# A second level of Strassen's algorithm for two of the seven products of a tiled GEMM, with a new order of its sums

## The chip, the cores and the metric

The kernel runs on one core of one Trainium2 chip. The metric is the device time of one execution in microseconds (us); for a comparison the median of several executions is taken. The core's engines are called as in the profile: PE is TensorE (matrix products), PEld its weight loads, DVE is VectorE, ACT is ScalarE, POOL is GpSimd, and SP issues the DMAs. Matrix products are written to banks of PSUM, the other tiles lie in SBUF.

## The reference

A retention recurrence over 4 sequences of 768 tokens and 8 heads of 64 gives a matrix x of 3072 x 512, and a layer with an ELU between two GEMMs follows. All is in 32 bits.

```
state = gamma[h] * state + outer(k[t], v[t])            # per sequence and head, 64 x 64
y[t]  = (q[t] @ state) / sqrt(64)
x     = y as (3072, 512)
h     = x @ w_in                                        # 512 x 2048
g     = where(h > 0, h, exp(min(h, 0)) - 1)
out   = g @ w_out                                       # 2048 x 512
```

## The kernel before

**Blocks.** The tokens go in six blocks (`tb` = 0 to 5) of 512. Block 0 is computed plainly (`plain_first`, `plain_second`), while the weights arrive and are decoded. From block 1 on both GEMMs use Strassen's algorithm in Winograd's form: the operands are cut into 2 x 2 quarters, and seven products M1 to M7 of combined quarters take the place of eight. The weights' combinations are made once (`combine_w_in` for the first GEMM, `combine_w_out` for the second), the inputs' once per block (`combine_x` makes four from `xb`, the retention's result).

**First GEMM.** `first(n)` computes a quarter of the hidden units, n = 0 to 3; in each, a product is four matmuls of 128x256 into one bank (line 497). `strassen` gives the order M1, M2, M6, M7, M5, M3, M4 and where the sums fall. Products that share a sum accumulate in one PSUM bank: M1, M6, M5 and M3 follow one another in bank `a`, and what stood there is taken out between two of them by a copy on ACT (`kept`, line 447). Bank `a` has two buffers, `b` and `d` one each. The sums C11, C12, C21 and C22 go through the ELU: two activations on ACT (lines 373 and 374) and one operation on DVE (line 376), which `elu` puts into the list `later`, so that it is issued with the next ELU. Combinations T1 and T3 of the results follow (line 509). The last two products of an n are run in the next n, or between products of the second GEMM.

**Second GEMM.** Block 1 uses `second`, one level of Strassen. Blocks 2 to 5 use `second_twice`: there every one of the seven products is itself cut into seven small products [1] to [7] of four matmuls of 128x128 each (line 618). The small weights come from DRAM through a ring of 11 buffers of 256 KB (`fetch_small`, lines 594 and 597), in the order of the list `to_fetch`: those that are quarters from `scratch`, those that are sums from `scratch2`, which `combine_w_out` filled during block 1. The ring and the inputs' pool `tpool` take the memory of the pools `stage` and `t4`, which are closed when block 1 is done. Between the products of the second GEMM the retention of the next block is done in five steps (`retention_step`), and its `combine_x` stands behind the last product's begin (`behind_last`).

**What sets the order.** The program is written in its final order; nothing reorders it. The generators `strassen`, `second_twice` and `inner` are stepped by hand in the loop at the end:

```
    for tb in range(1, NTB):
        for n in range(NQ):
            cur = first(n)
            for at in range(3):
                next(cur)
            for _ in tail:
                pass
            ...
            tail = cur
            if more:
                load((tb + 1) * CPB + n)
                scale_v((tb + 1) * CPB + n)
```

All DMAs are issued by SP in program order. Scaling v by the decay (`scale_v`, line 239) is POOL's only work from block 1 on.

Of the kernel before, what the change touches and what calls it, by code (L numbers as in the profile page):

```python
# [2 lines left out]

# [5 lines left out]
FP32 = mybir.dt.float32  # L9
# [3 lines left out]
ALU = mybir.AluOpType  # L13
# [3 lines left out]
def kernel(  # L17
# [3 lines left out]
    w_bits: bass.AP,  # L21
    scratch: bass.AP,
    scratch2: bass.AP,
    out: bass.AP,
    dims,
):

# [74 lines left out]

    w_a = [const.tile([P, 2, 2, 2, P], FP32, name=f"w_a{n}") for n in range(NQ)]
    w_b = [const.tile([P, 2, 2, 2, P], FP32, name=f"w_b{n}") for n in range(NQ)]
    w_s = [const.tile([P, 3, 2, 2, P], FP32, name=f"w_s{n}") for n in range(NQ)]
    NPIECE = 2 * NQ + NF  # L110
    staged, prepared, decoded = [], [], []

# [109 lines left out]


    xb = const.tile([P, 4, TB], FP32, name="xb")
    xt = [const.tile([P, 2, TH], FP32, name=f"xt{n}") for n in range(4)]
    carry = [const.tile([P, HP, D], FP32, name=f"carry{n}") for n in range(2)]
    held = {}

# [123 lines left out]

    half = [slice(0, TH), slice(TH, TB)]

    def combine_x():
        sub = lambda o, x, y: nc.vector.tensor_tensor(out=o, in0=x, in1=y, op=ALU.subtract)
        b11, b12, b21, b22 = (xb[:, 2 * r : 2 * r + 2, half[t]] for r in range(2) for t in range(2))
        sub(xt[0], b12, b11)
        sub(xt[1], b22, xt[0])
        sub(xt[2], b22, b12)  # L360
        sub(xt[3], b21, xt[1])


    later = []

    def flush():
        while later:
            later.pop(0)()

    def elu(g, h):  # L370

        r = epool.tile([P, 512], FP32, name="r", tag="r")
        nc.scalar.activation(r, h, AF.Relu, scale=-1.0)  # L373
        nc.scalar.activation(r, r, AF.Exp, scale=-1.0)  # L374
        flush()
        later.append(lambda: nc.vector.scalar_tensor_tensor(g, r, -1.0, h, ALU.add, ALU.max))  # L376

    def plain_first():

# [62 lines left out]
    def bank(x):  # L442
        return ps_f.tile([P, 2, TH], FP32, name="p" + x, tag=x, bufs=2 if x == "a" else 1)
# [103 lines left out]
                scratch2[j - 1, :, 1024 * k : 1024 * k + 1024], x.rearrange("p k f d -> p (k f d)")  # L547
            )

    def second(tb):  # L550
        def product(j, ps, begin):
            ws = fetched.pop((tb, j))
            for f in range(NF):
                for d in range(2):
                    nc.tensor.matmul(  # L555
                        ps[:, d, :], lhsT=ws[:, 2 * d + f // 4, f % 4, :], rhs=gq[INPUT2[j]][:, f, :],
                        start=(begin and f == 0 and d == 0), stop=(f == NF - 1), skip_group_check=True,
                    )
            at = ORDER2.index(j) + 3
            if j in (2, 6):  # L560
                next_input(j)
            combine_w_out(j, ws)
            if at < 7:
                fetch(tb, ORDER2[at])

        def use(name, h):
            r, t = int(name[1]) - 1, int(name[2]) - 1
            if name == "C12":
                ot = hpool.tile([P, 2, TH], FP32, name="h", tag="h")
                nc.scalar.copy(ot, h)  # L570
                h = ot
            nc.sync.dma_start(out[tb, r, t].rearrange("p d c -> p (d c)"), h.rearrange("p d c -> p (d c)"))

        return strassen(product, use, None)
# [1 line left out]


    RING = 11
    USE = [(1, k) for k in (1, 2, 6, 7, 5)]
    for at in range(1, 7):  # L580
        j, before = ORDER2[at], ORDER2[at - 1]
        USE += [(j, 1), (j, 2), (before, 3), (before, 4), (j, 6), (j, 7), (j, 5)]
    USE += [(4, 3), (4, 4)]
    to_fetch = [(tb, j, k) for tb in range(2, NTB) for j, k in USE]
    small_w = []

    def fetch_small():
        if not to_fetch:
            return
        tb, j, k = to_fetch.pop(0)  # L590
        t = ring.tile([P, 4, P], FP32, name="wq", tag="wq")
        if k in (1, 2, 4):
            q = 4 * SLOT[j] + {1: 0, 2: 1, 4: 3}[k]
            nc.sync.dma_start(t.rearrange("p f d -> p (f d)"), scratch[q])
        else:
            n = {5: 0, 6: 1, 7: 2, 3: 3}[k]
            nc.sync.dma_start(t.rearrange("p f d -> p (f d)"), scratch2[j - 1, :, 512 * n : 512 * n + 512])
        small_w.append(((tb, j, k), t))

    def second_twice(tb, behind_last):  # L600
        quarter = lambda x, r, t: x[:, 4 * r : 4 * r + 4, P * t : P * t + P]
        ts, kept2 = {}, {}

        def inputs(j):
            x, t = gq[INPUT2[j]], tpool.tile([P, 4, 4, P], FP32, name="ts", tag="ts")
            b11, b12, b21, b22 = (quarter(x, a, b) for a in range(2) for b in range(2))
            sub = lambda o, x, y: nc.vector.tensor_tensor(out=o, in0=x, in1=y, op=ALU.subtract)
            sub(t[:, 0], b12, b11)
            sub(t[:, 1], b22, t[:, 0])
            sub(t[:, 2], b22, b12)  # L610
            sub(t[:, 3], b21, t[:, 1])
            ts[j] = {1: b11, 2: b21, 3: b22, 4: t[:, 3], 5: t[:, 0], 6: t[:, 1], 7: t[:, 2]}

        def product(j, k, ps, begin):
            name, w = small_w.pop(0)
            assert name == (tb, j, k)
            for f in range(4):
                nc.tensor.matmul(  # L618
                    ps, lhsT=w[:, f, :], rhs=ts[j][k][:, f, :], start=(begin and f == 0), stop=(f == 3),
                    skip_group_check=True,  # L620
                )
            fetch_small()
# [9 lines left out]
        def inner(j):  # L632
            pool, tag = (mpool, "m") if j in (1, 6, 7, 5) else (hpool, "h")
            res = pool.tile([P, 2, 2, P], FP32, name="res", tag=tag)
            pa = bank("a")[:, 0, 0:P]
            product(j, 1, pa, True)
            m1 = copy(pa)
            pb = bank("b")[:, 0, 0:P]
            product(j, 2, pb, True)
            add(res[:, 0, 0], pb, m1)  # L640
            yield
            product(j, 6, pa, False)
            u2 = copy(pa)
            pd = bank("d")[:, 0, 0:P]
            product(j, 7, pd, True)
            yield
            product(j, 5, pa, False)
            add(res[:, 1, 1], pd, copy(pa))
            yield
            product(j, 3, pa, False)  # L650
            nc.scalar.copy(res[:, 0, 1], pa)
            product(j, 4, pd, False)
            add(res[:, 1, 0], pd, u2)
            sum_up(j, res.rearrange("p d t c -> p (d t c)"))
# [23 lines left out]
                add(m, kept2[7], m)  # L678
                store("C21", m)

        inputs(1)
        before = iter(())
        for at, j in enumerate(ORDER2):
            cur = inner(j)
# [3 lines left out]
            for _ in before:  # L688
                pass
            if j == 2:  # L690
                next_input(2)
            if j == 5:
                next_input(6)
# [12 lines left out]
            before = cur  # L706
            yield j
        for _ in before:
            pass


    prepare(2)
# [51 lines left out]
            for _ in combine_w_in(0):  # L764
                pass
    combine_x()
    for j in ORDER2[:3]:
        fetch(1, j)


    def retention_step(tb, step):
# [8 lines left out]
        elif step < 5:  # L780
            outputs_step(tb, step - 2)

    tail = iter(())
    for tb in range(1, NTB):
        more = tb + 1 < NTB
        for n in range(NQ):
            cur = first(n)
            for at in range(3):
                next(cur)

            for _ in tail:
                pass
            side = combine_w_in(n + 1) if tb == 1 and n + 1 < NQ else iter(())
            for s in cur:
                next(side, None)
                if s == "gap":
                    break
            for _ in side:
                pass
            tail = cur  # L800
            if more:
                load((tb + 1) * CPB + n)
                scale_v((tb + 1) * CPB + n)
        if tb == 1:
            cur = second(tb)
            next(cur)
            next(cur)
            for _ in tail:
                pass
            flush()  # L810
            for step, s in enumerate(cur):
                retention_step(tb + 1, step)
            combine_x()
            tail = iter(())
            early.close()
            ring = ctx.enter_context(tc.tile_pool(name="ring", bufs=RING))
            tpool = ctx.enter_context(tc.tile_pool(name="tpool", bufs=2))
            for _ in range(RING):
                fetch_small()
        else:  # L820
            cur = second_twice(tb, combine_x if more else lambda: None)
            next(cur)
            for s in tail:
                if s == "last":
                    break
            next(cur)
            for _ in tail:
                pass
            flush()
            for step, j in enumerate(cur):  # L830

                if step > 0:
                    retention_step(tb + 1, step - 1)
                if j == ORDER2[-1]:
                    break
            tail = cur
    for _ in tail:
        pass

# [45 lines left out]
```

## Time and profile before

| what | value |
|---|---|
| median of 10 runs | 665.61 us (662.45 to 667.54) |
| the profiled execution | 659.27 us, span 657.2 us |
| PE busy | 637.1 us, 97% of the span |
| DVE busy | 435.4 us, 66% |
| ACT busy | 228.3 us, 35% |
| POOL busy | 23.9 us, 4% |
| DMA moved | 123.64 MB, mean 188 GB/s |
| mean granted TensorE clock | 0.999 of full speed |
| first GEMM of block 2 | from 251.5 to 296.4 us |
| second GEMM of block 2, with the retention of block 3 | from 296.4 to 352.5 us |

The profile is that of one execution; its span runs from the first to the last instruction. Busy times of different engines overlap. A line such as `L618 PE MATMUL pa<-ts,wq 128*128 128x128` names the line of the kernel, the engine, the operation, the tile written and those read, the weights' shape and the result's. Each 32-bit matmul appears as two records. In a timeline the first number is the start and the second the length, both in us; matmuls are pipelined, so the difference between two starts is the time that one costs. In brackets stands how long the engine had been idle, and what released it.

### The profile page before, as it was taken

How to read it: one execution, taken by the hardware profiler on the slowest of the kernel's cores; microseconds unless marked ns; L12 is line 12 of the kernel's file. 1: busy time of each engine (PE TensorE's matmuls, PEld its weight loads, DVE VectorE, ACT ScalarE, POOL GpSimd, SP SyncE). 2: the span in 40 equal slices, each digit the busy share in tenths (PEclk: the TensorE clock that was granted, in tenths of full speed). 3: DMA queues.
4: the chain of work that ended last, by engine and by line, in shares of the span. 5: the costliest groups of instructions: out<-in, count | busy, mean ns of one | idle time of the engine just before them, and what ended most of it. 6: DMA issues, size and time to landing. Idle time of an engine off the chain costs nothing.

```text
span 657.2 us, 14662 instructions
## 1 busy us (share of the span) xinstructions
PE 637.1 (97%) x6144; PEld 537.3 (82%) x6144; DVE 435.4 (66%) x769; ACT 228.3 (35%) x432; POOL 23.9 (4%) x28
## 2 busy tenths in 40 slices
PE   4799999999999999999999999999999999999997
PEld 3664445458888888889999889999889999888996
DVE  5798688566767644558856548867447958345974
ACT  7477542005441002543112554112455111445211
POOL 1000100001100000200000200000200000000000
PEclk9999999999999999999999999999999999999999
DMA  8658977449114767604767602777801767200693
GB/s 337 242 165 292 339 228 235 143 132 380 74 63 152 255 222 246 266 1 160 239 211 247 253 1 95 231 231 250 302 2 44 238 214 265 94 1 27 217 306 125
DMA packets 63825, 123.64 MB, mean 188 GB/s; under 512 B 5136, under 2 KB 22544, under 8 KB 61712
## 3 DMA queue, kind: packets, MB, share of 16 engines
q1 hardware_dynamic: 63760, 122.70, 55.4%
q8 instruction: 49, 0.80, 0.5%
q14 instruction: 16, 0.13, 0.1%
HBM read 100.66 MB, written 22.02 MB: 187 GB/s over the span
## 4 chain that ended last, share of the span: by engine, by line
PE 94%; DVE 3%; DMA 1%; issue 1%; SPq 0%; ACT 0%; DVEq 0%
PE pa L497 21%; PE pa L618 15%; PE pd L497 11%; PE pd L618 8%; PE hp L396 6%; PE pb L497 5%; PE pa L410 4%; PE pa L555 4%; PE pb L618 4%; PE pd L555 2%; PE pb L410 2%; PE pd L410 2%; PE y L335 2%; PE sc L265 2%; PE y L311 2%; PE kv L287 2%
## 5 line engine op out<-in xcount | busy, mean ns | idle before, releaser
L452 DVE TENSOR_TENSOR h<-pd,m 128x512 f32<-128x512 f32 x42 | 29.0, 691 | 86.1 <-ACT m L447 68.6
L447 ACT COPY m<-pa 128x512 f32<-128x512 f32 x63 | 36.3, 576 | 109.7 <-PE pa L497 73.8
L626 ACT COPY ms<-pa 128x128 f32<-128x128 f32 x84 | 22.2, 265 | 123.9 <-PE pa L618 120.9
L374 ACT ACTIVATE r<-r 128x512 f32<-128x512 f32 x96 | 60.5, 630 | 3.1
L618 PE MATMUL pd<-ts,wq 128*128 128x128 f32 x448 | 59.9, 277 | 0.3 <-DVE res L630 0.3
L618 PE MATMUL pa<-ts,wq 128*128 128x128 f32 x448 | 59.2, 275 | 0.0
L373 ACT ACTIVATE r<-h 128x512 f32<-128x512 f32 x60 | 37.9, 631 | 57.2 <-DVE h L452 57.2
L618 PEld LDWEIGHTS pd<-ts,wq 128*128 128x128 f32 x448 | 54.5, 192 | 1.2 <-DVE res L630 0.9
L618 PEld LDWEIGHTS pa<-ts,wq 128*128 128x128 f32 x448 | 54.8, 192 | 0.2
L618 PE MATMUL pa<-gC,wq 128*128 128x128 f32 x384 | 52.0, 278 | 0.4 <-ACT ms L626 0.4
L376 DVE SCALAR_TENSOR_TENSOR gC<-r,h 128x512 f32<-128x512 f32 x60 | 42.5, 708 | 11.3 <-ACT r L374 11.3
L618 PEld LDWEIGHTS pa<-gC,wq 128*128 128x128 f32 x384 | 47.2, 192 | 1.7 <-ACT ms L626 0.5
L239 POOL TENSOR_TENSOR kvn<-kvn,vf 128x512 f32<-128x512 f32 x20 | 21.9, 1097 | 454.3 <-DMA kvn<-in_qkv_dram 448.9
L497 PE MATMUL pa<-xb,w_s 128*128 128x256 f32 x160 | 37.8, 379 | 0.0
L497 PE MATMUL pa<-xt,w_s 128*128 128x256 f32 x160 | 37.8, 379 | 0.0
L497 PE MATMUL pa<-xb,w_a 128*128 128x256 f32 x160 | 37.8, 379 | 0.0
L497 PE MATMUL pa<-xt,w_b 128*128 128x256 f32 x160 | 37.8, 379 | 0.0
L497 PE MATMUL pd<-xt,w_b 128*128 128x256 f32 x160 | 37.8, 379 | 0.0
L497 PE MATMUL pb<-xb,w_a 128*128 128x256 f32 x160 | 37.8, 379 | 0.0
L497 PE MATMUL pd<-xt,w_s 128*128 128x256 f32 x160 | 37.8, 379 | 0.0
L630 DVE TENSOR_TENSOR res<-pd,ms 128x128 f32<-128x128 f32 x56 | 16.1, 287 | 27.7 <-PE pd L618 25.3
L497 PEld LDWEIGHTS pa<-xt,w_b 128*128 128x128 f32 x160 | 30.4, 190 | 4.1
(121 smaller groups left out, 1093.0 us busy)
## 6 DMA issues: line engine op xcount, KB each, us to landing
wq<-scratch_dram SPq DMA_DIRECT2D x196, 256.0 KB, 4.0
wraw<-in_w_dram SPq DMA_DIRECT2D x16, 1024.0 KB, 6.0
qk<-in_qkv_dram SPq DMA_DIRECT2D x24, 512.0 KB, 8.9
kvn<-in_qkv_dram SPq DMA_DIRECT2D x24, 512.0 KB, 9.7
scratch_dram<-so SPq DMA_DIRECT2D x22, 512.0 KB, 3.4
ws<-scratch_dram SPq DMA_DIRECT2D x7, 1024.0 KB, 6.8
scratch_dram<-w_s SPq DMA_DIRECT2D x8, 512.0 KB, 7.3
out_dram<-res SPq DMA_DIRECT2D x12, 256.0 KB, 3.5
```

The lines of the kernel that those rows point to most:

```text
L239: eng.tensor_tensor(out=kv[:, 1], in0=kv[:, 1], in1=vf[:, i].unsqueeze(2).to_broadcast([C, H, D]), op=ALU.mult)
L373: nc.scalar.activation(r, h, AF.Relu, scale=-1.0)
L374: nc.scalar.activation(r, r, AF.Exp, scale=-1.0)
L376: later.append(lambda: nc.vector.scalar_tensor_tensor(g, r, -1.0, h, ALU.add, ALU.max))
L396: nc.tensor.matmul(hp, lhsT=w[n][:, fi, j // 2, j % 2, :], rhs=xb[:, j, :], start=(j == 0), stop=(j == 3))
L410: nc.tensor.matmul(ops[d], lhsT=wo[:, row, d * P : (d + 1) * P], rhs=g_plain[row * NF + f], start=(f == 0 and row == 0), stop=(f == NF - 1 ...
L447: nc.scalar.copy(m, ps)
L452: nc.vector.tensor_tensor(out=h, in0=ps, in1=m, op=ALU.add)
L497: nc.tensor.matmul(ps[:, fi, :], lhsT=w[:, fi, j2, :], rhs=x[:, j2, :], start=(begin and fi == 0 and j2 == 0), stop=(j2 == 1), skip_group_ ...
L555: nc.tensor.matmul(ps[:, d, :], lhsT=ws[:, 2 * d + f // 4, f % 4, :], rhs=gq[INPUT2[j]][:, f, :], start=(begin and f == 0 and d == 0), sto ...
L618: nc.tensor.matmul(ps, lhsT=w[:, f, :], rhs=ts[j][k][:, f, :], start=(begin and f == 0), stop=(f == 3), skip_group_check=True,)
L626: nc.scalar.copy(m, ps)
```

## The change

In blocks 2 to 5, the products M2 and M3 of the first GEMM are done with a second level of Strassen's algorithm, for all hidden units at once, ahead of the loop over n. The other five products stay in the loop.

- *Weights.* `combine_small` makes on POOL, during block 1, the four sums of quarters that M2 and M3 need, and stores them in a new DRAM tensor `scratch3`. The weights' tiles `w_a`, `w_b`, `w_s` and `xt` become single tiles with a leading index, so that one view runs over all n. Small weights that are plain quarters are read where they lie; sums come through the ring, eight a block.
- *Inputs.* `combine_x_twice` makes the small inputs of M2 and M3 where `combine_x` stood; `combine_x` itself is done in four parts during M2 and M3.
- *Products.* `first_twice(tb, j)` runs seven small products into the banks a, b and d and writes the four quarters of its result at once into the place of C11 (for M2) or C12 (for M3).
- *The loop over n.* M1, M6 and M5 accumulate in a bank `qa`, M7 and M4 in a bank `qd`, both from the pool `ps_r` that the retention uses at other times. `first_end` adds what is missing (for C11 and C12 the stored M2 and M3, for C22 and C21 a kept copy), writes the sum into g, and gives back the ELU to be issued later, which works in place from SBUF. Up to three ELUs are open, their ends are issued by `pop` at fixed places, and T3 and T1 hang on the end of C22.
- *Block 1.* `combine_w_in` is stepped twice per product, the loads for block 2 come at the head of each n, the scaling of v and the first three fetches for the second GEMM come behind the loop. The pools are exchanged and the ring's first fetches issued inside its last product (`change`).
- *Second GEMM.* The inputs of the first product are made in two parts, the first of them before M5 of n = 3; M4 of n = 3 stands between [1][2] and [6][7] of the first product; [3] and [4] of an inner product can be stepped apart.

The diff, cut to its core:

```diff
-    w_a = [const.tile([P, 2, 2, 2, P], FP32, name=f"w_a{n}") for n in range(NQ)]
...
+    w_a_, w_b_ = (const.tile([P, NQ, 2, 2, 2, P], FP32, name=x) for x in ("w_a", "w_b"))
+    w_s_ = const.tile([P, NQ, 3, 2, 2, P], FP32, name="w_s")
...
-    def elu(g, h):
-        r = epool.tile([P, 512], FP32, name="r", tag="r")
...
+    def elu(g, h, depth=1, then=None):
+        r = epool.tile([P, 512], FP32, name="r", tag="r", bufs=3)
...
+        def last():
+            nc.vector.scalar_tensor_tensor(g, e, -1.0, h, ALU.add, ALU.max)
+            if then:
+                then()
+        while len(later) >= depth:
+            later.pop(0)()
+        later.append(last)
...
+    TWICE = [2, 3]
+    SMALL = {5: 0, 6: 1, 7: 2, 3: 3}
...
+    W_IN = {2: w_a_[:, :, :, 1], 3: w_s_[:, :, 2]}
+    def combine_small(j):
+        t = stage.tile([P, 4, 4, P], FP32, name="wi", tag="stage")
...
+        tt = lambda o, x, y, op: nc.gpsimd.tensor_tensor(out=o, in0=x, in1=y, op=op)
+        tt(s1, a21, a22, ALU.add)
+        tt(s2, s1, a11, ALU.subtract)
+        tt(s3, a11, a21, ALU.subtract)
+        tt(s4, a12, s2, ALU.subtract)
+        nc.sync.dma_start(scratch3[j - 1], t.rearrange("p k f d -> p (k f d)"))
...
+    PLACE = {2: "C11", 3: "C12"}
+    def first_twice(tb, j):
...
+        def product(k, ps, begin):
...
+            for f in range(4):
+                nc.tensor.matmul(
+                    ps[:, f, :], lhsT=lhs[f], rhs=xs[j][k], start=(begin and f == 0), stop=True,
+                    skip_group_check=True,
+                )
+            if k in SMALL:
+                fetch_small()
...
+        pa = full(bank("a"))
+        product(1, pa, True)
+        m1 = lift(pa)
+        yield
+        pb = full(bank("b"))
+        product(2, pb, True)
+        plus(0, 0, pb, m1)
+        product(6, pa, False)
+        u2 = lift(pa)
+        pd = full(bank("d"))
+        product(7, pd, True)
+        m7 = lift(pd)
+        yield
+        product(5, pa, False)
+        plus(1, 1, pa, m7)
+        yield
+        product(4, pd, False)
+        plus(1, 0, pd, u2)
+        yield
+        product(3, pa, False)
+        lift(pa, place(dst, 0, 1))
...
+    def first_end(n, name, ps, x=None):
+        g = gq[name][:, 2 * n : 2 * n + 2, :]
+        nc.vector.tensor_tensor(out=g, in0=ps, in1=g if x is None else x, op=ALU.add)
...
+        return lambda: elu(g, g, 3, combine if name == "C22" else None)
...
     def second(tb, behind_last):
+            if j == 4:
+                behind_last()
...
-        inputs(1)
+        for _ in input_parts(1):
+            yield "input"
+        yield "inputs"
...
+    for n in range(NQ):
+        load(2 * CPB + n)
...
+        for j in smalls[n]:
+            combine_small(j)
+    for j in ORDER2[:3]:
+        fetch(1, j)
+    for m in range(2 * CPB, 3 * CPB):
+        scale_v(m)
+    def change():
...
+        for _ in range(RING):
+            fetch_small()
+        combine_x_twice()
...
+        rest(0, 1)
+        for _ in tail:
+            pass
+        tail, parts = iter(()), combine_x_parts()
+        for at, j in enumerate(TWICE):
+            cur = first_twice(tb, j)
+            next(cur)
+            next(tail, None)
+            next(parts, None)
+            next(cur)
+            for _ in tail:
+                pass
+            next(parts, None)
+            if at == 1:
+                first_end(0, "C11", qa[0])()
+            next(cur)
+            tail = cur
+        for _ in tail:
+            pass
...
+        for n in range(NQ):
+            first_rest(n, 6, qa[n])
+            u2[n] = kept(qa[n])
+            if end:
+                end()
+            pop()
+            pd[n] = ps_r.tile([P, 2, TH], FP32, name="qd", tag="r")
+            first_rest(n, 7, pd[n])
+            pop(2)
+            if n == 3:
+                next(sec)
+            first_rest(n, 5, qa[n])
+            u4 = kept(qa[n])
+            end = first_end(n, "C12", qa[n])
+            other = first_end(n, "C22", pd[n], u4)
+            end()
+            if n < 3:
+                other()
+                rest(n + 1, 1)
+                first_end(n + 1, "C11", qa[n + 1])()
+                first_rest(n, 4, pd[n])
+                end = first_end(n, "C21", pd[n], u2[n])
+                pop()
+                load_next(n + 1)
+            if more:
+                scale_v((tb + 1) * CPB + n)
+        for _ in range(2):
+            next(sec)
+        other()
+        first_rest(3, 4, pd[3])
+        end = first_end(3, "C21", pd[3], u2[3])
+        next(sec)
+        end()
+        flush()
```

## The prediction

> **What bounds the kernel now.** I read the page first: busy time, then the chain of waits.
>
> ```profile
> span 657.2 us, 14662 instructions
> PE 637.1 (97%) x6144; PEld 537.3 (82%) x6144; DVE 435.4 (66%) x769; ACT 228.3 (35%) x432; POOL 23.9 (4%) x28
> PE 94%; DVE 3%; DMA 1%; issue 1%; SPq 0%; ACT 0%; DVEq 0%
> ```
>
> TensorE is busy for 97% and is 94% of the chain. The list of waits gives it no regular wait behind its first microseconds. So this change is worth its TensorE time, less any gap it opens. The timeline at the end of token block 2's first GEMM has the prices (start, length, instruction):
>
> ```profile
> 294.62 1.89 PE L497 MATMUL pa<-xt,w_b 128*128 128x256 f32 x8
> 296.35 1.05 PE L618 MATMUL pa<-gC,wq 128*128 128x128 f32 x8
> 296.55 0.58 ACT L447 COPY m<-pa 128x512 f32<-128x512 f32 x1 [2.69 <-PE pa L497]
> 297.17 0.69 DVE L452 TENSOR_TENSOR h<-pd,m 128x512 f32<-128x512 f32 x1 [3.06 <-ACT m L447]
> 297.24 1.06 PE L618 MATMUL pb<-gC,wq 128*128 128x128 f32 x8
> 297.77 0.68 DVE L376 SCALAR_TENSOR_TENSOR gC<-r,h 128x512 f32<-128x512 f32 x1
> 299.86 1.89 PE L497 MATMUL pd<-xt,w_b 128*128 128x256 f32 x8
> 301.59 1.05 PE L618 MATMUL pa<-ts,wq 128*128 128x128 f32 x8
> 301.79 0.69 DVE L452 TENSOR_TENSOR h<-pd,m 128x512 f32<-128x512 f32 x1
> 302.54 1.16 PE L618 MATMUL pd<-ts,wq 128*128 128x128 f32 x8
> 303.53 1.06 PE L618 MATMUL pa<-ts,wq 128*128 128x128 f32 x8
> ```
>
> Starts are to be subtracted, since the printed lengths overlap. A 128x256 product (four matmuls, eight records) takes 296.35-294.62 = 1.727 us, a 128x128 product 297.24-296.35 = 0.893. ACT starts on a bank 0.20 after its last matmul; its copy takes 0.58, and DVE follows 0.04 later. A DVE operation takes 0.69, and the next may start 0.61 after it. At 301.59 a sum holds the bank that the next product needs: 0.893 of cover against 0.20+0.69 leaves TensorE 0.06 late (301.59+0.893 = 302.48, start 302.54), and the product after a wait takes 0.10 more (0.99). So a hand-over costs 0.20 before, 0.06 behind, and 0.10 for the restart.
>
> The table by windows shows the first GEMM of one block (columns: length; busy time of PE, PEld, DVE, ACT, POOL; granted clock, DMA share, GB/s):
>
> ```profile
> 251.50:296.40 44.90, 44.90 (x210) 39.53 (x209) 22.27 (x33) 21.61 (x37) 4.17 (x4) 1.00 0.46 164
> 296.40:352.50 56.10, 55.30 (x890) 53.73 (x889) 45.38 (x91) 11.40 (x34) 0.00 (x0) 1.00 0.67 215
> ```
>
> DVE and ACT are half idle there, TensorE never, at granted clock 1.00.
>
> **The change part by part.** I write M for a 128x256 product and [k] for a small one; the GEMM's halves are n = 0 to 3.
>
> *Fewer products.* For blocks 2 to 5, M2 and M3 were 4 x 1.727 = 6.91 us each and become seven small products, 7 x 0.893 = 6.25. Two per block, four blocks: 8 x 0.656 = 5.25 us saved.
>
> A rule speaks against this. "TensorE: Matmul & The Clock Gate", Back-to-back issue gap, in the Trainium skill says that in a stream of weight loads and matmuls a matmul takes about 81 ns at 128 columns and 131 at 512: halving the columns hardly helps. My interpolation gives some 98 ns at 256; small products would then be 28 x 81 against 16 x 98, 45% dearer: +3.1 us each, +25 us in all. The row here is 111.6 ns a record at 128 columns against 215.9 at 256, a ratio of 0.517, with a weight load before each as in the new code. I take the row.
>
> *New work on ACT and DVE.* Per block: six DVE sums for M2 and M3, four more at the joins (C12 was read from its bank, now M3 is added from SBUF), four of 256 elements for the new inputs (0.42, by the 128x256 rows), so some 8.6 us; ACT has eight copies more and four fewer, +2.3. Window DVE 22.3 becomes 31, ACT 24, in some 43.6 us of TensorE. It all lies beside TensorE unless order makes it late, so I walked the queues.
>
> *Inside M2 and M3.* Products run [1][2][6][7][5] of M2; [1] of M3; [4] of M2; [2][6][7]; [3] of M2; [5][4][3] of M3. [6] needs the copy of [1], with only [2] between: 0.20+0.58+0.06 = 0.84 against 0.893, and [5] of M2 likewise behind [7]. Both fit by 0.05; two per block, costed at 0. If ACT were late by 0.2, each would be 0.25: 2 us in all. Pre-existing SBUF traffic doesn't slow ACT in the rows, hence 0. The end doesn't fit. With [3] of M2 ending at T: ACT lifts it by T+0.78; DVE makes C11 of n = 0 at T+0.82, since it needs that quarter; behind it in DVE's order, the sum for [5] of M3 runs T+1.43 to T+2.12. TensorE has done [5] and [4] at T+1.79 and can start [3] at T+2.18. Wait 0.39 and restart 0.10: 0.49 x 4 = 1.96 us.
>
> *The n loop.* Five products, 8.64 us per n. M4 needs C22's sum: M5's end, 0.20, copy 0.58, 0.04, sum 0.69, 0.06 = 1.57, covered by M1 of the next n (1.73). DVE per n: four sums at 0.65, four ELU ends at 0.70, T3 and T1 at 1.4, so 6.8 of 8.64 (79%). In order: the last ELU end popped before M5's end is that of C21; its exponential ends some 3.8 us behind M6's start, the ELU end at 4.6, and M5 ends at 5.18, so C12's sum is not late. Cost 0. At n = 3 two input subtractions (1.2) are put ahead of C12's sum: it starts 0.4 late, C22's sum ends 1.90 behind M5, and the cover is only [1][2] of the second GEMM, 1.79. With 0.06 and 0.10: 0.27 x 4 = 1.08 us. The old stall there (302.54) goes, because [7] no longer takes a bank that M4 just left: -0.16 x 4 = -0.64.
>
> *Scaling v on POOL* remains four operations a block, each beside some n. These rows show what it does to DVE:
>
> ```profile
> 163.37 1.52 POOL L239 TENSOR_TENSOR kvn<-kvn,vf 128x512 f32<-128x512 f32 x1 [1.52 <-DMA kvn<-in_qkv_dram]
> 163.91 1.53 DVE L431 TENSOR_TENSOR w_s<-w_a,w_b 128x512 f32<-128x512 f32 x1
> 272.99 0.69 DVE L452 TENSOR_TENSOR h<-pd,m 128x512 f32<-128x512 f32 x1 [2.79 <-ACT m L447]
> 273.00 1.04 POOL L239 TENSOR_TENSOR kvn<-kvn,vf 128x512 f32<-128x512 f32 x1 [1.52 <-DMA kvn<-in_qkv_dram]
> ```
>
> DVE operations on two SBUF inputs can lose 0.84, those on a PSUM bank nothing. The ELU ends have 0.78 in hand (4.6 to 5.38), so 0.
>
> *Block 1.* combine_w_in moves two blocks' work into n = 0; DVE was idle from about 149.9 to 155.0 except for two of its operations, so 0. POOL gets eight operations for the combined quarters. They can start when the last w_s is made, by my reckoning near 168.3: at 1.04 each POOL ends at 176.6, at the contended 1.52 at 180.5. SP runs in order: the three fetches of the second GEMM, issued at 146.90 before, are now queued behind both stores of these quarters. A 1 MB fetch lands after 6.8 us by the page, so by 183.4 to 187.3, and block 1's second GEMM needs it at 190.57. Cover 3 to 7 us: 0. Beyond 1.8 us per POOL operation, each 0.1 would cost 0.8. The loads, moved to the head of each n, and the v scalings, moved behind POOL's quarters, are needed only from 207.8 on: 0.
>
> *Entry to block 2.* The ring's first fetches went at 252.81, with 43 us to spare; now [6] of M2 needs one 1.73+2x0.893 = 3.51 us behind block 1's last product (251.46). They wait for the last weights' buffer, so go near 251.5; quickest landing in that stretch 2.8 us, at 254.3 against 254.97. The subtractions for [6] wait for the store issued at 249.1 (2.7 us): ready near 253. Bounds: 0 and, at the stretch's median landing of 6.2, +2.7. The queue is empty at that moment, so I take nearer the lower: 0.3. Later blocks fetch eight small weights more (2 MB), from a ring eleven deep: 0.
>
> *Sum:* -5.25+1.96+1.08-0.64+0.3 = -2.55. The profiled execution took 659.27 (span 657.2, 2.07 around it): it becomes 656.7, span 654.65. The median of the runs shown, 665.61, lies 6.3 above that execution; the same step gives 663.1.
>
> **The rivals.**
> 1. *Everything hidden*: the waits I found overlap slack I didn't count, and only the saved products count: -5.25 and the old 0.64, 660. For it: the clean hand-overs of before. Against: the C11 order is written in the code.
> 2. *Entry costs eat it*: late ring fetches (+2.7) or POOL slower than contended: some 2 to 4 us given back once, 664.5 to 667. Against: the empty queue at 251.5 and 3 us of cover.
> 3. *DVE becomes the bound of the n loop: slower.* At 79%, in order, with ELU ends that wait for ACT in front of the sums that free the banks, a late queue makes each M4 late. Place: C12's sum behind M5, sixteen times. It decides when M4 waits (4.55/16)-0.10 = 0.18 us each, which needs DVE some 0.9 later than walked (0.58+0.20 spare, 0.16 slack at M4, then the wait). At 0.4 late: 16 x 0.5 = 8 us, less 2.55: 671. For it: 31 of 43 us and contention with POOL. Against: POOL touches only four n in a block, not the sums.
> That the small products don't run at 0.893 (other weights, strided views) would be seen first; each keeps 128 columns in a row, so I give it nothing of its own.
>
> **How the numbers follow.** Forecast 0.58 (661 to 665.2), rival 1 0.16, rival 2 0.12, rival 3 0.14. A measurement of this kernel tells 0.3%, 2 us, from no change. Faster: three quarters of the forecast (0.45) and rival 1: 0.61. Same: 0.13, 0.10 of rival 2, 0.01 of rival 3: 0.24. Slower: 0.15. The range 659.8 to 667.8 leaves out most of rival 3 and the tail of rival 1.
>
> **What would show it.** Right: M2 and M3 of blocks 2 to 5 as 0.893 us steps; per block one wait of about 0.4 of the last small product of M3 on a DVE sum, and one of 0.2 at M4 of n = 3; a span near 654.7. Wrong: steps over 0.95 between all small products; M4 waiting on DVE in every n; TensorE waiting for ws near 190 or for wq near 255; any new wait over 1 us.

## The result: slower, by the wait that the prediction had costed at nothing

The changed kernel takes 668.50 us (median of 14 runs, 666.35 to 671.31) against 663.85 us for the kernel before in the same comparisons (49 runs, 660.84 to 667.54). The ratio is 1.0067 (95%: 1.005 to 1.0084), that is +3.3 to +5.6 us, where -2.55 had been predicted. It is slower by more than the 0.3% that a measurement can tell.

Three rows of the changed kernel's page (those of before stand in the prediction):

```profile
span 666.5 us, 15234 instructions
PE 639.8 (96%) x6336; PEld 540.2 (81%) x6336; DVE 467.4 (70%) x825; ACT 238.2 (36%) x448; POOL 38.0 (6%) x36
PE 83%; DVE 11%; DMA 2%; issue 2%; ACT 1%; SPq 0%; DVEq 0%
```

TensorE is still busy for 96%, so the first row of engines says little. The chain of waits says more: DVE had 3% of it and has 11%. Yet DVE works for only 70% of the span, so it isn't the bound; TensorE waits for it at certain places. The list of waits names them (five of its rows; columns: engine, tile and line that wait, for what; us in total, times, longest):

```profile
PE sc L269 <- DMA qk<-in_qkv_dram: 8.9, 2, 7.5
PE qd L736 <- DVE gC L744: 4.3, 16, 0.5
PE kv L291 <- issue: 2.2, 2, 1.7
PE pa L690 <- DVE gC L704: 0.8, 4, 0.2
PE pa L690 <- DMA wq<-scratch_dram: 0.2, 1, 0.2
```

The first was there before the change (9.1). The second is new: M4 (bank `qd`) waits 16 times, once for each n of each of blocks 2 to 5, for a DVE sum. The fourth is the wait of [3] of M3 and the fifth the entry to block 2, both predicted. The timeline of the loop over n in block 2, at n = 1, shows what M4 waits for:

```profile
280.96 1.89 PE L736 MATMUL qa<-xt,w_b 128*128 128x256 f32 x8
282.68 1.89 PE L736 MATMUL qa<-xb,w_a 128*128 128x256 f32 x8
282.88 0.59 ACT L467 COPY m<-qa 128x512 f32<-128x512 f32 x1 [1.68 <-PE qa L736]
283.50 0.69 DVE L744 TENSOR_TENSOR gC<-qa,gC 128x512 f32<-128x512 f32 x1 [0.40 <-ACT m L467]
284.11 0.68 DVE L744 TENSOR_TENSOR gC<-qd,m 128x512 f32<-128x512 f32 x1
284.85 1.99 PE L736 MATMUL qd<-xt,w_b 128*128 128x256 f32 x8 [0.27 <-DVE gC L744]
286.68 1.89 PE L736 MATMUL qa<-xt,w_s 128*128 128x256 f32 x8
```

M5 fills bank `qa` from 280.96 and is done at 282.68. ACT copies the bank to `m` from 282.88. C12's sum (`gC<-qa,gC`) reads the same bank and nothing that ACT makes: `m` isn't among its operands. DVE is idle, and still the sum starts only at 283.50, after 0.40 of idle time put down to that copy. C22's sum, which does need `m`, stands behind it in DVE's order and starts at 284.11. M4 needs its bank, could have started at 282.68+1.727 = 284.41, starts at 284.85, and takes 286.68-284.85 = 1.83 instead of 1.727. That is 0.44+0.10 us.

At n = 1 DVE was busy with ELU ends until 283.10, so 0.40 is all that the copy cost the sum there. At n = 0 DVE had long been idle, and the sum still starts 0.62 behind the start of the copy:

```profile
273.71 0.58 ACT L467 COPY m<-qa 128x512 f32<-128x512 f32 x1 [2.87 <-PE qa L736]
274.33 0.69 DVE L744 TENSOR_TENSOR gC<-qa,gC 128x512 f32<-128x512 f32 x1 [5.60 <-ACT m L467]
```

In eleven of the twelve cases of n = 0 to 2 DVE idles like this, for 0.40 to 5.60 us, and M4 starts 0.44 late each time. The twelfth (n = 1 of block 3) is 0.24 worse: an ELU end that ran beside POOL's scaling of v took 1.53 us instead of 0.68 and kept DVE busy until 1.14 behind M5.

The window of the whole first GEMM of block 2 (length; busy time of PE, PEld, DVE, ACT, POOL; granted clock, DMA share, GB/s) shows that neither DVE nor ACT is full, nor is the clock lower:

```profile
253.20:301.00 47.80, 46.62 (x265) 41.31 (x264) 30.11 (x48) 24.21 (x41) 4.69 (x4) 1.00 0.56 198
```

DVE has 30.11 of 47.80 us, near the 31 that had been reckoned, and idles for a third of the time.

Comparing times of this size needs care: two profiled executions of one kernel differ by as much. The kernel before took 659.27 us in its first and 663.89 in a second profile (`before_again`); the changed one took 668.28 and 673.77 (`after_again`). The executions with the longer times show more waits put down to nothing ("issue"):

```profile
PE sc L265 <- issue: 2.7, 2, 1.4
PE kv L287 <- issue: 2.0, 1, 2.0
PE y L311 <- issue: 0.8, 1, 0.8
```

These three are of the second profile of before and make 5.5 us; its first has 0.9, 0.8, 0.6 and 0.5. So steps are compared by the length of a block's first GEMM, which repeats to a few hundredths in the kernel before and to 0.24 in the changed one, worked out from the timelines of TensorE (from M1 of n = 0 to [1] of the second GEMM, us). Before, M3 of n = 3 lay behind that [1]; the third column adds its 1.73.

| kernel | block 2 | block 3 | block 3 with M3 | block 4 | block 5 |
|---|---|---|---|---|---|
| before | 44.89 | 46.68 | 48.41 | 46.69 | 46.68 |
| before, second profile | 44.90 | 46.69 | 48.42 | 46.68 | 46.69 |
| changed | 47.85 | 49.52 | 49.52 | 49.30 | 49.29 |
| changed, second profile | 47.73 | 49.28 | 49.28 | 49.29 | 49.29 |

By the two first profiles the four blocks' first GEMMs (block 2 with 1.73 more as well) have grown by 1.23+1.11+0.89+0.88 = 4.1 us, where 0.8 less in each had been reckoned (-1.31 for the products, +0.49 for [3] of M3).

### The profile page after: what moved, and what is told of

It reads as the page before. It is cut to its first block, busy times and chain, and to the rows that moved or that the text cites. A ratio compares the mean times of both kernels' runs of the same rounds, so it can differ in the third digit from the quotient of the medians.

```text
span 666.5 us, 15234 instructions
## 1 busy us (share of the span) xinstructions
PE 639.8 (96%) x6336; PEld 540.2 (81%) x6336; DVE 467.4 (70%) x825; ACT 238.2 (36%) x448; POOL 38.0 (6%) x36
## 4 chain that ended last, share of the span: by engine, by line
PE 83%; DVE 11%; DMA 2%; issue 2%; ACT 1%; SPq 0%; DVEq 0%
PE pa L775 13%; PE qd L736 8%; PE pd L775 7%; PE qa L736 7%; PE hp L416 6%; PE pa L430 4%; PE pa L575 4%; PE pa L517 4%; PE pa L690 4%; DVE gC L744 4%; PE pb L775 3%; DVE gC L390 2%; PE kv L291 2%; PE pd L575 2%; PE pd L517 2%; PE y L339 2%
## 5 line engine op out<-in xcount | busy, mean ns | idle before, releaser
L744 DVE TENSOR_TENSOR gC<-qa,gC 128x512 f32<-128x512 f32 x32 | 22.0, 687 | 36.3 <-ACT m L467 29.6
L386 ACT ACTIVATE r<-gC 128x512 f32<-128x512 f32 x64 | 40.0, 625 | 15.4 <-DVE gC L744 15.4
L390 DVE SCALAR_TENSOR_TENSOR gC<-r,gC 128x512 f32<-128x512 f32 x64 | 43.1, 710 | 0.7 <-ACT r L387 0.7
L736 PE MATMUL qd<-xt,w_b 128*128 128x256 f32 x128 | 31.9, 392 | 4.3 <-DVE gC L744 4.3
L652 DVE TENSOR_TENSOR ts<-gC,ts 128x512 f32<-128x512 f32 x48 | 33.0, 688 | 0.8
L736 PEld LDWEIGHTS qd<-xt,w_b 128*128 128x128 f32 x128 | 23.0, 189 | 12.4 <-DVE gC L744 9.9
L652 DVE TENSOR_TENSOR ts<-gC 128x512 f32<-128x512 f32 x48 | 32.8, 683 | 0.0
L430 PE MATMUL pa<-gC,w_s 128*128 128x512 f32 x64 | 30.6, 600 | 0.0
L736 PE MATMUL qa<-xt,w_s 128*128 128x256 f32 x128 | 30.2, 379 | 0.0
L736 PE MATMUL qa<-xb,w_a 128*128 128x256 f32 x128 | 30.2, 379 | 0.0
```

The source lines that it names most:

```text
L386: nc.scalar.activation(e, h, AF.Relu, scale=-1.0)
L390: nc.vector.scalar_tensor_tensor(g, e, -1.0, h, ALU.add, ALU.max)
L430: nc.tensor.matmul(ops[d], lhsT=wo[:, row, d * P : (d + 1) * P], rhs=g_plain[row * NF + f], start=(f == 0 and row == 0), stop=(f == NF - 1 ...
L736: nc.tensor.matmul(ps[:, fi, :], lhsT=w[:, fi, j2, :], rhs=x[:, j2, :], start=(j in (1, 7) and fi == 0 and j2 == 0), stop=(j2 == 1), skip_ ...
L744: nc.vector.tensor_tensor(out=g, in0=ps, in1=g if x is None else x, op=ALU.add)
```

## The experiments

All are edits of the changed kernel. In the expectations R is the theory that came from the timeline: two engines that read one PSUM bank do so one behind the other, in program order, and so C22's sum comes late. The other theories are its rivals; each expectation says what they would give. M5 counts as done when the next product starts.

**C22's sum first** (`e1_c22_first`). If R holds, C12's sum costs nothing where it follows C22's: it has no bank that M4 needs.

```diff
             u4 = kept(qa[n])
-            end = first_end(n, "C12", qa[n])
             other = first_end(n, "C22", pd[n], u4)
+            end = first_end(n, "C12", qa[n])
```

> Edit: in the loop over n the sum of C22 is issued ahead of the sum of C12. Theory R (two engines that read the same bank are put in order: C12's sum on DVE waits for the copy u4 on ACT, though it doesn't use it, and C22's sum stands behind it): C22's sum then ends 0.20+0.59+0.04+0.69+0.06 = 1.58 us behind M5, inside the 1.73 of the next M1, so the waits of M4 at n = 0 to 2 go (12 x 0.53 = 6.4 us) and that at n = 3 (4 x 0.48 = 1.9): about 660 us, 8 below the changed kernel, some 3 to 4 below the one before. Theory D (DVE is too full in the loop, the prediction's third rival): the work stays the same, M4 or M6 goes on waiting, less than 3 us gained. Theory S (the small products themselves cost what was saved): no change of the waits elsewhere, so at most the same as R.

Measured: 660.97 us (median of 22 runs, before 664.23), ratio 0.9956 (0.9942 to 0.9969). The timeline at the same place:

```profile
282.02 1.89 PE L736 MATMUL qa<-xb,w_a 128*128 128x256 f32 x8
282.22 0.59 ACT L467 COPY m<-qa 128x512 f32<-128x512 f32 x1 [1.31 <-PE qa L736]
282.84 0.69 DVE L744 TENSOR_TENSOR gC<-qd,m 128x512 f32<-128x512 f32 x1 [0.46 <-ACT m L467]
283.44 1.28 DVE L744 TENSOR_TENSOR gC<-qa,gC 128x512 f32<-128x512 f32 x2
283.74 1.89 PE L736 MATMUL qd<-xt,w_b 128*128 128x256 f32 x8
```

C22's sum starts 0.82 behind M5 instead of 1.43, and M4 follows after 1.72 without a wait, at 1.89 and not 1.99. None of the 16 waits is left. By the two ratios the two lines are worth (1.0067-0.9956) x 664 = 7.4 us; the 12 x 0.53 and 4 x 0.48 of the trace make 8.3. Block 3 takes 47.67. The prediction's terms for that block, with the 0.10 that the hand-overs inside M2 measured and without the wait, give 48.41-1.31+0.49+0.10 = 47.69.

**The copy behind C12's sum** (`e2_copy_behind`). If only ACT's copy were slow, moving it would change little for DVE; if readers go in program order, the copy must now wait for the sum.

```diff
-            u4 = kept(qa[n])
             end = first_end(n, "C12", qa[n])
+            u4 = kept(qa[n])
             other = first_end(n, "C22", pd[n], u4)
```

> Edit: the copy u4 on ACT is written behind the sum of C12 in the program, nothing else is moved. Theory R: readers of one bank follow each other in program order, so now the copy waits for the sum: it starts about 0.93 us behind M5 and not 0.20, C22's sum ends at 0.20+0.69+0.04+0.58+0.04+0.69+0.06 = 2.30, and M4 waits 0.57 where it waited 0.43; about 2 us slower than the changed kernel. If there is no order between readers and only DVE is late: the copy still starts 0.20 behind M5, C12's sum as well, C22's sum ends near 1.6, and M4's wait goes (6 us faster).

Measured: one run of 674.05 us, too few for a ratio. Timeline at n = 2 of block 2, where DVE is idle when M5 ends, and list of waits:

```profile
292.30 1.89 PE L736 MATMUL qa<-xb,w_a 128*128 128x256 f32 x8
292.50 0.69 DVE L744 TENSOR_TENSOR gC<-qa,gC 128x512 f32<-128x512 f32 x1 [0.63 <-PE qa L736]
293.23 0.58 ACT L467 COPY m<-qa 128x512 f32<-128x512 f32 x1 [2.40 <-DVE gC L744]
293.85 0.69 DVE L744 TENSOR_TENSOR gC<-qd,m 128x512 f32<-128x512 f32 x1 [0.65 <-ACT m L467]
294.59 1.99 PE L736 MATMUL qd<-xt,w_b 128*128 128x256 f32 x8 [0.40 <-DVE gC L744]
```

```profile
PE qd L736 <- DVE gC L744: 10.7, 16, 1.4
```

The bank had been full since 292.30 and ACT idle for 2.40, but the copy starts 0.93 behind M5, as R had it, and 0.73 behind the start of the sum, to which its wait is put down. The order of the two readers has turned round with the program. M4 is 0.56 late here, where it was 0.44. With e1 this shows the cause: the order of two readers of one bank. Both read the whole tile; whether readers of two tiles in one bank would also wait for each other, no run here shows.

The blocks take 48.98, 50.59, 49.74 and 49.74 us, 3.1 more in all than in the first profile of the changed kernel, where 2 was expected for the whole: at n = 1 of blocks 2 and 3 an ELU end beside POOL's scaling delays both readers, and M4 is 1.4 to 1.5 late. At n = 3 (1.1 late) another thing shows:

```profile
301.81 0.69 DVE L652 TENSOR_TENSOR ts<-gC,ts 128x512 f32<-128x512 f32 x1
302.42 0.68 DVE L744 TENSOR_TENSOR gC<-qa,gC 128x512 f32<-128x512 f32 x1
```

M5 ended at 301.60. C12's sum is the first reader of its bank here and still starts 0.82 behind M5, since DVE is busy with the second input's subtraction.

**One level for M2 and M3** (`e3_one_level`). Is the second level worth what was reckoned? M2 and M3 are done here as plain products at the same place, and ACT copies them to C11 and C12; all else stays.

```diff
-            cur = first_twice(tb, j)
+            cur = first_once(tb, j)
```
```
    def first_once(tb, j):
        for n in range(NQ):
            ...
            for fi in range(2):
                for j2 in range(2):
                    nc.tensor.matmul(ps[:, fi, :], lhsT=w[:, fi, j2, :], rhs=x[:, j2, :], ...)
            nc.scalar.copy(gq[PLACE[j]][:, 2 * n : 2 * n + 2, :], ps)
            yield
```

> Edit: M2 and M3 of blocks 2 to 5 are done with one level again, 16 products of 128x256 in place of 28 of 128x128 each, in the same place ahead of the loop and with the same loop behind them; the eight small weights a block are not fetched. Theory R (the loop over n loses the time): TensorE +8 x 0.656 = 5.25 us, less the wait of [3] of M3 (4 x 0.49) and the hand-overs between ACT and the small products (about 0.4) and the entry to block 2 (0.4): about 2.5 us slower than the changed kernel, 671; the waits of M4 stay at 0.43. Theory S (the small products lose the time): faster than the changed kernel, near the kernel before.

Measured: 672.75 us (6 runs), ratio 1.0154 (1.0123 to 1.0185). The wait of M4 stays (the edit shifts the lines):

```profile
PE qd L749 <- DVE gC L757: 4.1, 16, 0.3
```

So the wait doesn't hang on the small products. The stretch from M1 of n = 0 to M6 of n = 0, in blocks 3 to 5, takes 17.33 here and 16.59 in the changed kernel: 0.74 us less per block with the second level. The reckoned 1.31 less the 0.49 of [3] of M3 and 0.10 for the hand-overs is 0.72. The second level is worth what the prediction said; four blocks make 3.0 us. The whole times differ by (1.0154-1.0067) x 664 = 5.8, and the two intervals leave anything from 2.6 to 9.

**C11's sum later** (`e4_c11_later`). In the changed kernel, at the end of M3, C11's sum of n = 0 stands ahead of the sum of [5], whose bank the last small product needs:

```profile
265.37 0.58 ACT L700 COPY gC<-pa 128x512 f32<-128x512 f32 x1 [0.31 <-PE pa L690]
265.99 0.69 DVE L744 TENSOR_TENSOR gC<-qa,gC 128x512 f32<-128x512 f32 x1 [1.70 <-ACT gC L700]
266.60 0.68 DVE L704 TENSOR_TENSOR gC<-pa,m 128x512 f32<-128x512 f32 x1
267.33 1.16 PE L690 MATMUL pa<-xb,wq 128*128 128x128 f32 x8 [0.21 <-DVE gC L704]
```

This is as it had been walked: 0.62 from the copy's start to C11's sum, 0.61 to the next sum, and the product after it late.

```diff
+            next(cur)
             if at == 1:
                 first_end(0, "C11", qa[0])()
-            next(cur)
```

> Edit: the sum and ELU of C11 of n = 0 are issued behind the sum for [5] of M3, not ahead of it. The prediction's step: the 0.49 us wait of [3] of M3 goes in each of four blocks, 2.0 us faster than the changed kernel (666.5), and M6 of n = 0 doesn't wait, since C11's sum ends 2.4 us behind [3] of M2 and M6 starts 3.6 behind it. Rival: the wait only moves to M6 or to M5 of n = 0, no gain.

Measured: 667.60 us (9 runs), ratio 1.0056 (1.0033 to 1.008), which can't be told from the changed kernel. The place itself:

```profile
265.54 1.06 PE L690 MATMUL pd<-ts,w_s 128*128 128x128 f32 x8
265.81 0.69 DVE L704 TENSOR_TENSOR gC<-pa,m 128x512 f32<-128x512 f32 x1 [2.05 <-PE pa L690]
266.56 1.16 PE L690 MATMUL pa<-xb,wq 128*128 128x128 f32 x8
```

The sum is early now, at 0.27 behind the end of [5], but 0.27+0.69+0.06 = 1.02 of hand-over against 0.893 of cover still leaves 0.13 and the restart: 266.56-265.54 = 1.02, and 1.00 for the product that follows. The wait shrinks from 0.48 to 0.24, a gain of 1.0 us in four blocks where 2.0 was expected. The miss is mine: one small product doesn't cover a DVE hand-over here.

**C22 first, and two products of cover** (`e5_order`). e1, and in M3 [5] is stepped ahead of [3] of M2, C11's sum behind; the order of the fetches follows.

```diff
             next(cur)
+            if at == 1:
+                next(cur)
             for _ in tail:
                 pass
             next(parts, None)
             if at == 1:
                 first_end(0, "C11", qa[0])()
-            next(cur)
+            else:
+                next(cur)
             tail = cur
```

> Edit: C22's sum ahead of C12's as in e1, and in M3 the small product [5] is run ahead of [3] of M2 (its sum then ahead of C11's on DVE). e4 showed that moving only the sum leaves 0.23 us of the 0.49, since one product of 0.893 cannot cover 0.20+0.07+0.69+0.06. Theory: now two products, 1.79 us, lie between [5] and [3] of M3, and C11's sum ends 1.57 us behind [3] of M2 against 1.79 of cover for M6: the wait goes wholly, 4 x 0.49 = 2.0 us less than e1's 661.0, less 0.05 per block for the now tight copy ahead of [5]: 659.2. Rival: the wait turns up at [5] (its copy) or at M6 of n = 0: e1's time.

Measured: 658.99 us (6 runs, before 664.59), ratio 0.9919 (0.9887 to 0.9951). This version beats both kernels. Timeline of the end of M3:

```profile
263.75 1.10 PE L690 MATMUL pa<-ts,wq 128*128 128x128 f32 x8
264.69 1.06 PE L690 MATMUL pa<-xb,wq 128*128 128x128 f32 x8
264.96 0.69 DVE L704 TENSOR_TENSOR gC<-pa,m 128x512 f32<-128x512 f32 x1 [1.80 <-PE pa L690]
265.58 1.06 PE L690 MATMUL pd<-ts,w_s 128*128 128x128 f32 x8
266.47 1.06 PE L690 MATMUL pa<-xb,wq 128*128 128x128 f32 x8
```

[5] at 263.75, then [3] of M2 and [4] of M3 cover its sum, and [3] of M3 follows at 0.89. The stretch of M2 and M3 takes 16.16, 0.43 less than in the changed kernel. A whole first GEMM takes 47.42 and 47.41 in blocks 3 and 4, only 0.26 less than in e1, and 47.25 in block 5. In blocks 2 to 4 of this profile an ELU end at n = 1 ran beside POOL's scaling, 1.53 us instead of 0.68; C22's sum started 0.24 later for it, and M4 lost 0.17. What still waits at the head of the second GEMM is there in e1 as well: [6] of its first product for 0.23, behind an ACT copy, and [2] of its second for 0.16, behind an ELU end.

**The end of n = 3** (`e6_order_n3`, then `e7_elu_only`). Both are e5 and a move of the ELU of C12 of n = 3 behind the first copy of the second GEMM; e6 also issues T3 and T1 of n = 3 behind the ELU end of C21.

```diff
             end = first_end(n, "C12", qa[n])
-            end()
             if n < 3:
+                end()
                 other()
...
         for _ in range(2):
             next(sec)
+        end()
         other()
```

> Edit: e5, and at n = 3 the ELU of C12 is issued behind the first copy of the second GEMM, and T3 and T1 of n = 3 behind the end of C21's ELU. Theory: what is left in e1 around n = 3 goes: [6] of the second GEMM's first product waits for its ACT copy behind two activations (0.23 a block), [2] of the next product waits for C21's end behind T3 and T1 on DVE (0.16): 4 x 0.39 = 1.6 us less than e5, 657.6. Rival: ACT is the limit there and C21's ELU comes as late as before: only the 0.23 goes, 658.3.

Measured, e6: 659.69 us (13 runs), ratio 0.9937 (0.9916 to 0.9957). Neither 657.6 nor the rival's 658.3 came, and no gain over e5 can be told; a wait that e5 has twice is there six times:

```profile
PE pd L775 <- DVE res L787: 2.3, 6, 0.4
```

The four more, 0.43 each, are [7] of the second product, whose bank is freed by a small sum that now stands behind the two subtractions T3 and T1. To tell whether the subtractions or the ELU did it, e7 moves the ELU alone.

> Edit: e5 and only the first of e6's two edits (at n = 3 the ELU of C12 behind the first copy of the second GEMM); T3 and T1 stay ahead of the end of C21's ELU. In e6 a new wait of 0.43+0.10 a block stood at [7] of the second product, behind a small sum on DVE that had moved behind T3, T1 and the inputs. If T3 and T1 made it, it is gone here, [6]'s 0.23 is gone too, and [2] keeps its 0.16: 4 x 0.23 = 0.9 us less than e5, about 658. If the moved ELU made it, the wait is still there: 659.5 as in e6.

Measured, e7: 659.42 us (6 runs), ratio 0.9935 (0.9915 to 0.9956), not to be told from e5, where about 658 was expected. The list of waits has

```profile
PE pd L775 <- DVE res L787: 0.6, 2, 0.4
```

again, so T3 and T1 made the new wait. [6]'s wait is gone as well, but that of [2] grows from 0.16 to 0.29. Behind the C22 order, a move at this place mostly hands a wait to the next product.

**Both kernels once more** (`before_again`, `after_again`), for what varies between executions.

> The kernel before, profiled once more. Its profile (659.3) lay under all its timed runs but the changed one's did not, and in the first 42 us the changed kernel's profile is 1.7 us behind though nothing was changed there. If that belongs to the execution, this profile reaches the first 128x512 product nearer to 41.9 than to 40.1 us and its blocks 2 to 5 take as long as before (405.7 us from 251.5 to the end), within 1 us. If it belongs to the code, it is at 40.1 again.

> The changed kernel, profiled once more, for the same question: the waits of M4, 0.43+0.10 in n = 0 to 2 and 0.38+0.10 in n = 3, come back to 0.02 us if they are the program's; the time to the first 128x512 product and the waits that the profile puts down to nothing (2.2+1.0+0.6 us) may differ by 1 to 2 us if they are the execution's.

Measured: 663.89 and 673.77 us. The new wait of M4 comes back as it was:

```profile
PE qd L736 <- DVE gC L744: 4.3, 16, 0.5
PE kv L291 <- issue: 3.8, 2, 2.1
PE pa L775 <- issue: 1.4, 1, 1.4
```

So do the lengths of the first GEMMs (table above), but for the ELU end beside POOL's scaling: its 0.24 is in block 2 here and was in block 3. Blocks 2 to 5 of before as a whole don't repeat within the 1 us that was expected: 409.4 us instead of 405.7. What differs are the "issue" waits, 2.8 and 5.8 us in the two profiles of before, 3.8 and 6.2 of the changed kernel, and the start-up: the first product of 128x512 starts at 40.14 and 41.23 before, at 41.87 and 42.07 after. From there to M1 of block 2 both kernels take 211.3 us in each of their profiles, so what was moved inside block 1 costs nothing.

## Why the prediction was wrong

The account of the change by the starts in its profile, step by step, against the terms of the sum:

| step | predicted, us | measured, us |
|---|---|---|
| fewer products | -5.25 | -5.25 (0.893 each) |
| hand-overs to ACT within M2 | 0 | 7 x 0.05 = 0.35 |
| [3] of M3 behind C11's sum | 4 x 0.49 = 1.96 | 4 x 0.48 = 1.9 |
| M4 in the loop, n = 0 to 2 | 0 | 12 x 0.53 = 6.4 |
| an ELU end beside POOL's scaling (block 3) | 0 | 0.24 |
| M4 at n = 3 | 4 x 0.27 = 1.08 | 4 x 0.48 = 1.9 |
| [2] of the second product of the second GEMM | not named | 4 x 0.29 = 1.2 |
| a wait in the last block's second GEMM, 0.40 and not 0.16 | not named | 0.24 |
| old stall | -0.64 | -0.64 |
| entry to block 2 | 0.3 | 0.4 |
| POOL's quarters, SP's queue, block 1 | 0 | 0 |
| sum | -2.55 | +6.7 |

**The failed step** is the hand-over in "The n loop": "M4 needs C22's sum: M5's end, 0.20, copy 0.58, 0.04, sum 0.69, 0.06 = 1.57, covered by M1 of the next n". It leaves out that C12's sum stands between the copy and C22's sum on DVE. The prediction had looked at that sum, but only for lateness in DVE's queue ("so C12's sum is not late"): its terms hold only if C12's sum starts at once behind M5, beside the copy, and is over when the copy is. It starts 0.62 later, and at n = 0 and 2, where DVE is free before M5 ends, by the order of the bank's readers alone. The row becomes 0.20+0.59+0.03+0.61+0.69+0.05 = 2.17 against 1.73 of cover: 0.44 and the restart. e1 and e2 show this cause by taking it away and turning it round. One of the prediction's signs of being wrong, M4 waiting on DVE in every n, is what came.

At n = 3 the prediction had C22's sum end 1.90 behind M5, with the sum of C12 0.4 late; the profile has it later:

```profile
301.03 1.05 PE L775 MATMUL pa<-gC,wq 128*128 128x128 f32 x8
301.92 1.06 PE L775 MATMUL pb<-gC,wq 128*128 128x128 f32 x8
302.45 0.68 DVE L744 TENSOR_TENSOR gC<-qd,m 128x512 f32<-128x512 f32 x1
303.19 1.99 PE L736 MATMUL qd<-xt,w_b 128*128 128x256 f32 x8 [0.21 <-DVE gC L744]
```

M5 ends at 301.03, C22's sum at 302.45+0.68 = 303.13, 2.10 behind it. Here the bank isn't needed to explain it: the copy and the second input's subtraction let C12's sum go at the same time, 0.82 behind M5, and in e2 the subtraction alone held it as long. What the prediction had too small at n = 3 is the place of that subtraction in DVE's queue, by 0.2.

The Trainium skill states the rule that would have led there, in "PSUM — Partial Sum Buffer", section "PSUM bank collisions raise a hardware error ⚠️": two engines may not be at the same bank and the same 32 partitions in the same cycle, reads against reads included, so that the compiler puts a dependency between any two instructions of different engines on one bank, ACT against DVE too. The trace agrees: C12's sum starts 0.62 us behind the copy, with DVE idle for 5.60 before it (274.33 against 273.71). A collision itself no run here shows, nor what put the order into this program. The prediction did not weigh this rule. From the trace of before it took the gap between a copy and the sum that uses it, not one between two readers that share nothing but the bank.

**The small products were right.** Their 0.893 held in every block, and e3 shows the second level to be worth 0.74 us a block with its costs, 0.72 by the sum. The rule on the issue gap that spoke against the change would have made it 25 us slower; the row was the better guide.

**The wait of [3] of M3** was right to 0.1 us in its sum (1.9 against 1.96), and so was what hides the work on POOL and SP in block 1: no wait near 190, none for `ws`. The entry cost 0.33+0.07 instead of 0.3. The 0.78 in hand of the ELU ends against POOL's scaling didn't always do: once in each of the two profiles, at n = 1, it cost 0.24.

**[2] of the second product** was never looked at. It reads C21, whose ELU end stands on DVE behind T3 and T1, and takes 1.18 instead of 0.89:

```profile
308.48 0.68 DVE L390 SCALAR_TENSOR_TENSOR gC<-r,gC 128x512 f32<-128x512 f32 x1
308.59 1.34 PE L775 MATMUL pb<-gC,wq 128*128 128x128 f32 x8
309.77 1.06 PE L775 MATMUL pa<-gC,wq 128*128 128x128 f32 x8
```

**Hand-overs with 0.05 to spare** cost 0.05 each and not 0: where ACT frees the bank after 0.84 and the product lasts 0.893, the next one took 0.94.

**The rivals.** Rival 3 had the place, sixteen times M4, and nearly the price (16 x 0.5 = 8 us), but not the cause. At n = 0 to 2 DVE wasn't late with its queue but once, by 0.24; it stood idle for 0.40 to 5.60 ahead of C12's sum. So its test, how far DVE lags, looked at the wrong thing, and that its price came near is luck; at n = 3 a late queue explains the wait as well as the bank does. Rivals 1 and 2 are excluded by the waits: 16 new ones at M4, and 0.4 in all at the entry.

**What stays open.** The account gives +6.7 us, the medians +4.65 (3.3 to 5.6). Within the first GEMMs the account agrees with the table: -5.25+0.35+1.9+6.4+0.24+0.4 = 4.0 against 4.1. It leaves out the start-up and the "issue" waits, which the medians contain, and which differ by 3.0 and 2.4 us between two profiles of the same kernel. The whole times of the two pairs of profiles differ by 9.0 and 9.9, more than the account, and so don't help. Whether the remaining 2 us between account and medians are that, or something that the change speeds up elsewhere, wasn't settled. Nor was what the "issue" waits are.

## What to carry to other kernels

When a sum is walked through the queues, count the readers of each PSUM bank as one queue more, in program order, across engines (here ACT and DVE); a reader that shares no operand can still be waited for. Of two readers, issue first the one whose result frees the bank that TensorE needs next, and put the other behind it. Before relying on a cover, add up the whole hand-over: here a DVE sum needs 0.20 to 0.27, 0.69 and 0.06, which a product of 0.893 doesn't cover and one of 1.73 does.

## What the runs showed of the hardware

- A second reader of a bank, on the other engine, started 0.62 us behind the start of an ACT copy (0.58 long), and 0.73 behind that of a DVE sum (0.69 long, in e2): one read ended before the other began, in either order.
- The DVE sum that cost TensorE 0.44 us and a restart of 0.10 at each n = 0 to 2 cost nothing when it was issued one place later (e1), with the same work on every engine.
- A DVE operation on two SBUF inputs (an ELU end) took 1.53 us beside POOL's scaling and 0.68 otherwise.
- Waits of TensorE that the profile puts down to nothing took 2.8 to 6.2 us per execution: 3.0 of the 4.6 us between the two profiles of before, 2.4 of the 5.5 between those of the changed kernel.
